# A local and pooled attention with a dense pair behind it: the new form from pair 8, with work moved between engines

## The chip, the cores and the metric

The kernel runs on one core of a Trainium2 chip. TensorE (PE in the profile; its weight loads are PEld) multiplies matrices, VectorE (DVE) and GpSimd (POOL) work elementwise, ScalarE (ACT) does copies and functions, and SyncE (SP) issues the DMAs. The metric is the time of one execution on the device in microseconds, as the median of three runs.

## The reference

There are 8 batches with 8 heads, 576 positions and head size 64. Two attentions are computed and added, and their sum, laid out as 4608 tokens of 512 features, goes through two matrix products with an elementwise function between them.

```python
q_d = q.reshape(B, H, Sd, factor, D).mean(axis=3)   # factor 4: 144 pooled positions; k_d, v_d alike
out_d = sm_attn(q_d, k_d, v_d)                      # softmax attention over the pooled positions
out_up = np.repeat(out_d, factor, axis=2)
mask = np.abs(pos[:, None] - pos[None, :]) < factor # a band of 7 positions
out_local = np.matmul(attn, v)                      # softmax of q k^T / 8 inside that band
x = (out_up + out_local) as [4608, 512]             # token by head and feature
h = x @ w_in;  g = h - np.tanh(h);  out = g @ w_out # 512 -> 2048 -> 512
```

## The kernel before

**Tiling.** Two heads of one batch make a pair; there are 32 pairs, four to a batch, and a batch is a block of 576 tokens. `attention(p)` handles a pair. The local attention works on five tiles of about 112 queries by 128 keys; the pooled attention on 5 groups of 32 pooled positions. For each pair, in order:

- loads of q, k and v (`load_qk`, `load_v`), two or four DMAs on SP, into four and five buffers;
- casts to bf16: `qr` (L443, one per head, on VectorE, ScalarE or GpSimd) and `vw` (L383);
- the transposition of q and k into `qk`, features on partitions. In the old form (`TIN` is 'pe') nine TensorE transposes (L466) into the score bank `ps_ts`, and two copies out of it (L474, ScalarE or VectorE). In the new form (`TIN` is 'dma') one DMA transpose (L448) from `qr` to `qT`, and two reorders of `qT` (L455, ScalarE);
- the pooled q and k: two additions, `half` (L486) and `qkd` (L495);
- the scores (L504) and pooled scores (L526), in two steps in the score bank, or where `MERGE` holds in one step over the score bank and the product bank `ps_ox`;
- exponents (L544, L555, L558) and, from pair 4, masks (L548 for 912 columns, L562 for 240);
- the products with V (L573) and pooled V (L579) into `ps_ox`, reciprocals and normalising (L588, L590) into `ln`;
- the way into `xT`, features on partitions again. In the old form (`XOUT` is 'pe') twelve TensorE products (L601, L604) and one copy (L632). In the new form one DMA transpose (L607) and a join of two additions (L619, L623).

`pool_v` pools V for two pairs: five products (L398, L400) and a copy (L405).

**The dense part.** `mm1` computes 128 of the 2048 inner features for 512 tokens (even blocks) or 320 (odd blocks): four products over the four head pairs (L662), tanh on ScalarE (L670) into `u`, and a subtraction on VectorE (L673) into `gT`. `mm2` multiplies `gT` with `w_out` (L690); a finished tile of 128 tokens is copied to `y` (L704) and stored (L707). `dense(kb)` interleaves `mm1` of block kb with `mm2` of block kb - 1; for kb 1 all of `mm2(0)` goes first. Block 0's attention runs by itself; from then on the attention of later pairs runs between the dense products.

**PSUM.** Eight banks: `ps_ts` (scores) and `ps_ox` (products), two banks each; in block 0 a second pair of the same, `ps_ts1` and `ps_ox1`, and after block 0 in their place four separate dense banks `ps_hy`.

**What sets the order.** Every step is recorded as an operation with an engine (or a choice of engines), a cost in ns, the keys that it reads and writes, and a priority. `Program.order` is a list planner: it starts on each engine the operation with the lowest priority number among those that are ready, and takes for a choice the engine that is free first. On SP at most eight DMAs are in flight. A result counts as ready for another engine after a latency (`LAT`: 230 ns from TensorE, 1800 ns from a DMA). Operations with priorities from `SPARE[0]` = 119 (pairs from 12, since the priority is ten times the pair) get a further margin: 600 ns ahead of TensorE, 1500 ns behind a DMA. TensorE's dense products have priority 5000 and fill what attention leaves free. The instructions are then issued on each engine in this order; what the planner took too short becomes a wait. Where the plan shows a longer idle time of TensorE in block 0, warm-up products (L824) on a zero tile are put in.

The constants that decide the forms stand at the end of the kernel:

```python
EARLY, BIASED = 12, 4
TIN = ['pe'] * EARLY + ['dma'] * (NPAIR - EARLY)
MERGE = [False] * EARLY + [True] * (NPAIR - EARLY)
XOUT = ['pe'] * EARLY + ['dma'] * (NPAIR - EARLY)
```

Of the kernel before, what the change touches and what calls it, by code (L numbers as in the profile page):

```python
# [8 lines left out]
FP32 = mybir.dt.float32  # L9
BF16 = mybir.dt.bfloat16  # L10
AF = mybir.ActivationFunctionType
ALU = mybir.AluOpType
PSUM = bass.MemoryType.PSUM


class Program:
# [8 lines left out]
    SPARE = 119, {"PE": 600, "ACT": 0, "DVE": 0, "DMA": 1500}  # L25
# [140 lines left out]
def kernel(  # L166
# [13 lines left out]
    NP = H // 2  # L180
    NPAIR = B * NP
# [54 lines left out]
    ps_hy = []  # L236


    early = ExitStack()
    psum_e = early.enter_context(tc.tile_pool(name="psum_e", bufs=1, space=PSUM))  # L240
    ps_ts1 = fixed("ps_ts1", [128, 2, 512], FP32, pool=psum_e)
    ps_ox1 = fixed("ps_ox1", [128, 2, 512], FP32, pool=psum_e)

    def dense_banks():
        early.close()
        pool = ctx.enter_context(tc.tile_pool(name="psum_d", bufs=1, space=PSUM))
        ps_hy.extend(fixed("ps_hy", [128, 512], FP32, 4, pool=pool))
# [141 lines left out]
    def pool_v(hb):  # L389

        w = hb % NVW
        pri = 20 * hb - 1
        bank, keys = (ps_ox, ["ox"]) if 2 * hb < NP else (ps_ts, [("ts", 0)])
        pv = bank[:, 0, :].rearrange("p (w c) -> p w c", w=2)

        def mm():
            for t in range(4):
                T.matmul(pv[32 * t:32 * t + 32, 0, :], pick[:, 0:32],  # L398
                         vw[w][:, :, t, 0:64], start=True, stop=True)
            T.matmul(pv[:, 1, :], pick[:, 32:160], vw[w][:, :, 4, 0:64],  # L400
                     start=True, stop=True)
        P.fresh.add(len(P.ops))
        op("PE", 350, mm, reads=[("vw", w, 0), ("vw", w, 1), "pick"],
           writes=keys, pri=pri)
        op("ACT", 470, lambda: A.copy(  # L405
            out=vd[w][:, :, :, 0:64],
            in_=pv.rearrange("p w (h d) -> p w h d", d=D)),
           reads=keys, writes=[("vd", w)], pri=pri)


    def attention(p):
# [27 lines left out]
        else:  # L439
            for hh in range(2):  # L440
                dst = qr[s][:, :, hh]
                srt = qkn[sn][:, hh].rearrange("p (a d) -> p a d", d=D)
                P.choice([(eng, ns, lambda dst=dst, srt=srt, fn=fn: fn(out=dst, in_=srt))  # L443
                          for eng, ns, fn in any3],
                         reads=[("qkn", sn, 0), ("qkn", sn, 1)],
                         writes=[("qr", s, hh)], pri=pri - 12)
        if TIN[p] == 'dma' and LOAD[p] == 'row':
# [6 lines left out]
            for i in range(2):  # L454
                op("ACT", 1080, lambda i=i: A.copy(  # L455
                    out=full[:, i].rearrange("p (g a) -> p g a", a=A9),
                    in_=qT[s][:, :, i::2].rearrange("p a g -> p g a")),
                   reads=[("qT", s)], writes=[("qk", s, i)], pri=pri)
# [88 lines left out]
        if not biased:  # L547
            op("DVE", 700, lambda: V.tensor_tensor(  # L548
            out=e1, in0=e1,
            in1=mask[:, 0:456].unsqueeze(1).to_broadcast([128, 2, 456]),  # L550
            op=ALU.mult), reads=["mask"], writes=[("E", s, 0)], pri=pri)
# [9 lines left out]
        if not biased:  # L561
            op("DVE", 300, lambda: V.tensor_tensor(  # L562
            out=e2v, in0=e2v,
            in1=mask[:, 456:576].unsqueeze(1).to_broadcast([128, 2, 120]),
            op=ALU.mult), reads=["mask"], writes=[("E", s, 1)], pri=pri)


# [38 lines left out]
        if XOUT[p] == 'dma':  # L606
# [21 lines left out]
            P.choice([("DVE", 800, lambda: join(V)), ("POOL", 1300, lambda: join(GP))],  # L628
# [8 lines left out]
    slots = [0, 1, 2, 3]  # L637
# [13 lines left out]
    def mm1(kb, i):  # L651
        t0, n, parts = span(kb)
        fc, g, c0 = i // parts, kb % 2, n * (i % parts)
        slot, us = take(), un[0] % 3
        un[0] += 1
        bs = sorted({(t0 + c0) // S, (t0 + c0 + n - 1) // S})

        def mm(part):
            if not ps_hy:
                dense_banks()  # L660
            for dc in range(2 * part, 2 * part + 2):
                T.matmul(ps_hy[slot][:, 0:n], w_in_sb[:, dc, fc * 128:(fc + 1) * 128],  # L662
                         xT[dc][:, t0 + c0:t0 + c0 + n],
                         start=(dc == 0), stop=(dc == N_DC - 1))
        for part in range(2):
            op("PE", 27 * n // 32, lambda part=part: mm(part),
               reads=[("w_in", fc // 4, c) for c in range(4)] +
               [("x", b, j) for b in bs for j in range(NP)],
               writes=[("hy", slot)], pri=5000)
        op("ACT", 90 + 76 * n // 100, lambda: A.activation(  # L670
            out=u[us][:, 0:n], in_=ps_hy[slot][:, 0:n], func=AF.Tanh),
           reads=[("hy", slot)], writes=[("u", us)], pri=-1)
# [3 lines left out]
           reads=[("hy", slot), ("u", us)], writes=[("gT", g, fc)], pri=-1)  # L676
# [4 lines left out]
    def mm2(kb, i):  # L681
# [16 lines left out]
        if part == 3:  # L698
# [5 lines left out]
            op("ACT", 480, lambda: A.copy(out=y[ys], in_=ps_hy[slot]),  # L704
               reads=[("hy", slot)], writes=[("y", ys)], pri=-1)
# [3 lines left out]
               reads=[("y", ys)], writes=[("yq", ys)], pri=-1)  # L709
# [15 lines left out]
    EARLY, BIASED = 12, 4  # L725
# [3 lines left out]
    XOUT = ['pe'] * EARLY + ['dma'] * (NPAIR - EARLY)  # L729
# [3 lines left out]
    LATE = 8  # L733
    T_QK, T_QKN, T_V, T_W, NEARLY = 840, 1350, 690, 2850, NP
# [121 lines left out]
```

## Time and profile before

| | |
|---|---|
| runs (us) | 338.45, 337.45, 338.14; median 338.14 |
| profiled execution (us) | 339.43, of which the span is 337.70 |
| granted TensorE clock | 1.00 |
| busy in the span (us) | TensorE 323.9, ScalarE 244.0, VectorE 213.4, GpSimd 130.8 |
| DMA | 58.15 MB, mean 172 GB/s |

The profile's page gives busy times, slices of the span, the chain of work that ended last, and groups of instructions with their idle time before them and what ended it. A row of a window shows the stretch, its length, and then per engine the busy time and the number of instructions (PE, PEld, DVE, ACT, POOL). A row of the chain is start, length, what ran. A row of the timeline is start, length, engine, line, operation, tiles, form, and in brackets the idle time before it with what ended it. A matmul's length includes its passage through the array; the distance between two starts is what it holds the engine.

### The profile page before, as it was taken

Reading aid. Unit: us, or ns where it says so; the run is one execution under the profiler, and the core shown is the slowest. Engines: PE = TensorE matmul, PEld = TensorE weight load, DVE = VectorE, ACT = ScalarE, POOL = GpSimd, SP = SyncE. Lnnn points to the kernel's source line nnn. Section 1 sums busy time; section 2 is a strip of 40 time slices with the busy share of each in tenths; the row PEclk is TensorE's granted clock in tenths of the full one; section 3 lists DMA queues with packets and bytes.
Section 4 is the critical chain, followed back from the end, with each engine's and each line's share of the span. In section 5 each row is a group of like instructions: output and inputs, shape, how many; then the busy total and the mean of one; then the engine's idle time right before and its main releaser. Section 6 shows DMA issues by size and latency. Waiting matters only on the chain.

```text
span 337.7 us, 7262 instructions
## 1 busy us (share of the span) xinstructions
PE 323.9 (96%) x2736; PEld 179.2 (53%) x2736; DVE 213.4 (63%) x401; ACT 244.0 (72%) x434; POOL 130.8 (39%) x176
## 2 busy tenths in 40 slices
PE   6898999989999999999799999999999999999995
PEld 2464455557664454566465445565664444665542
DVE  6577784558886788678578776786764333455200
ACT  3786896489998988998799999998654334554311
POOL 5644655574444464365375655645110000000000
PEclk9999999999999999999999999999999999999999
DMA  7999999866689999999999974453220100100021
GB/s 211 321 391 324 358 386 321 243 189 163 152 237 188 222 216 255 206 211 245 216 244 234 240 144 99 95 105 76 58 61 31 63 32 33 60 34 31 33 92 64
DMA packets 102979, 58.15 MB, mean 172 GB/s; under 512 B 86048, under 2 KB 86048, under 8 KB 102944
## 3 DMA queue, kind: packets, MB, share of 16 engines
q1 hardware_dynamic: 102944, 57.69, 65.0%
q8 instruction: 21, 0.34, 0.4%
q14 instruction: 14, 0.11, 0.1%
HBM read 37.75 MB, written 9.44 MB: 140 GB/s over the span
## 4 chain that ended last, share of the span: by engine, by line
PE 83%; ACT 5%; DVE 4%; DMA 4%; issue 1%; POOL 1%; SPq 0%; ACTq 0%; POOLq 0%
PE ps_hy L690 36%; PE ps_hy L662 33%; PE ps_ts L504 3%; PE ps_ox L573 3%; PE ps_ox L579 2%; ACT qk L474 2%; DVE qk L474 2%; PE ps_ts L466 2%; DMA lT<-ln 1%; DMA vst<-in_v_dram 1%; DMA qkn<-in_k_dram 1%; PE ps_ts L398 1%; PE ps_ts L400 1%; PE ps_ox L526 1%; PE ps_ox L604 1%
## 5 line engine op out<-in xcount | busy, mean ns | idle before, releaser
L662 PE MATMUL ps_hy<-xT,w_in_sb 128*128 128x320 bf16 (+1 forms) x768 | 147.0, 326 | 2.8 <-DVE gT L673 1.9
L690 PE MATMUL ps_hy<-w_out_sb,gT 128*128 128x512 bf16 x576 | 144.2, 379 | 0.0
L673 DVE TENSOR_TENSOR gT<-ps_hy,u 128x320 bf16<-128x320 f32 (+1 forms) x192 | 102.6, 552 | 59.2 <-ACT u L670 57.6
L670 ACT ACTIVATE u<-ps_hy 128x320 f32<-128x320 f32 (+1 forms) x192 | 92.3, 501 | 45.9 <-PE ps_hy L662 41.4
L662 PEld LDWEIGHTS <-w_in_sb 128*128 128x128 bf16 x768 | 72.3, 98 | 56.4 <-issue 3.1
L690 PEld LDWEIGHTS <-gT 128*128 128x128 bf16 x576 | 54.1, 98 | 53.9
L486 POOL TENSOR_TENSOR half<-qk 128x576 f32<-128x576 bf16 x31 | 36.1, 1166 | 40.5 <-ACT qk L455 25.3
L455 ACT COPY qk<-qT 128x576 bf16<-128x576 bf16 x40 | 48.1, 1219 | 0.0
L383 POOL CAST vw<-vst 128x640 bf16<-128x640 f32 x30 | 21.9, 734 | 40.4 <-PE ps_ox L573 40.1
L544 ACT ACTIVATE E<-ps_ts 128x912 bf16<-128x912 f32 x32 | 29.8, 932 | 9.1 <-PE ps_ts L504 7.5
L704 ACT COPY y<-ps_hy 128x512 f32<-128x512 f32 x36 | 21.3, 593 | 20.1 <-PE ps_hy L690 20.0
L590 DVE TENSOR_TENSOR ln<-ps_ox,r 128x896 bf16<-128x896 f32 x32 | 34.9, 1090 | 1.0
L443 POOL CAST qr<-qkn 128x576 bf16<-128x576 f32 x34 | 24.3, 727 | 20.8 <-PE ps_ts L466 16.8
L548 DVE TENSOR_TENSOR E<-E,mask 128x912 bf16<-128x912 bf16 x28 | 20.9, 748 | 10.4 <-ACT E L544 10.0
L495 POOL TENSOR_TENSOR qkd<-half 128x320 bf16<-128x320 f32 x28 | 21.7, 776 | 1.5
L573 PE MATMUL ps_ox<-vw,E 128*128 128x65 bf16 x320 | 19.3, 194 | 0.0
L573 PEld LDWEIGHTS <-E 128*128 128x128 bf16 x320 | 16.2, 98 | 5.6
L579 PE MATMUL ps_ox<-vd,E 128*128 128x65 bf16 x256 | 18.0, 193 | 0.1
L504 PEld LDWEIGHTS <-qk 64*128 64x128 bf16 x320 | 9.4, 95 | 15.8 <-issue 14.8
L588 DVE RECIPROCAL r<-ps_ox 128x14 f32<-128x14 f32 x32 | 7.7, 241 | 15.4 <-PE ps_ox L579 15.4
L504 PE MATMUL ps_ts<-qk 64*128 64x112 bf16 (+1 forms) x280 | 14.9, 216 | 1.0 <-DVE qk L474 1.0
L474 ACT COPY qk<-ps_ts 128x512 bf16<-128x512 bf16 (+1 forms) x14 | 10.2, 744 | 6.4 <-DVE qk L474 3.9
(75 smaller groups left out, 262.9 us busy)
## 6 DMA issues: line engine op xcount, KB each, us to landing
vst<-in_v_dram SPq DMA_DIRECT2D x64, 160.0 KB, 4.4
qkn<-in_q_dram SPq DMA_DIRECT2D x32, 288.0 KB, 4.1
qkn<-in_k_dram SPq DMA_DIRECT2D x32, 288.0 KB, 4.4
out_dram<-y SPq DMA_DIRECT2D x36, 256.0 KB, 2.3
gT<-in_moe_w_in_dram SPq DMA_DIRECT2D x4, 1024.0 KB, 10.0
xT<-in_moe_w_out_dram SPq DMA_DIRECT2D x8, 256.0 KB, 5.2
gT<-in_moe_w_out_dram SPq DMA_DIRECT2D x2, 1024.0 KB, 8.3
qT<-qr SPq DMA_TRANSPOSE x20, 3.5
```

The lines of the kernel that those rows point to most:

```text
L443: P.choice([(eng, ns, lambda dst=dst, srt=srt, fn=fn: fn(out=dst, in_=srt)) for eng, ns, fn in any3], reads=[("qkn", sn, 0), ("qkn", sn, 1 ...
L455: op("ACT", 1080, lambda i=i: A.copy(out=full[:, i].rearrange("p (g a) -> p g a", a=A9), in_=qT[s][:, :, i::2].rearrange("p a g -> p g a") ...
L486: eng.tensor_tensor(out=half, in0=four[:, :, :, 0:2], in1=four[:, :, :, 2:4], op=ALU.add)
L504: T.matmul(out, qk[s][rows, 1, KW * t:KW * t + 128], qk[s][rows, 0, Q0[t]:Q0[t] + NQ[t]], start=not biased, stop=not biased or t >= 3)
L544: op("ACT", 820, lambda: A.activation(out=e1, in_=ps[:, :, 0:456], func=AF.Exp, scale=SCALE), reads=ts, writes=[("E", s, 0)], pri=pri)
L573: T.matmul(po[:, hh, 65 * t:65 * t + 65], E[s][:, c:c + 128], vw[w][:, 2 * jj + hh, t, :], start=True, stop=True)
L579: T.matmul(po[:, hh, o:o + 65], E[s][:, c + GW * i:c + GW * i + 128], vd[w][:, i, 2 * jj + hh, :], start=(i == 0), stop=(i == 1))
L590: op("DVE", 1010, lambda: V.tensor_tensor(out=ln[s].rearrange("p n (h d) -> p h n d", d=D), in0=blocks[:, :, :, 0:64], in1=r[s].unsqueeze( ...
L662: T.matmul(ps_hy[slot][:, 0:n], w_in_sb[:, dc, fc * 128:(fc + 1) * 128], xT[dc][:, t0 + c0:t0 + c0 + n], start=(dc == 0), stop=(dc == N_DC ...
L670: op("ACT", 90 + 76 * n // 100, lambda: A.activation(out=u[us][:, 0:n], in_=ps_hy[slot][:, 0:n], func=AF.Tanh), reads=[("hy", slot)], writ ...
L673: op("DVE", 70 + 105 * n // 100, lambda: V.tensor_tensor(out=gT[g][:, fc, c0:c0 + n], in0=ps_hy[slot][:, 0:n], in1=u[us][:, 0:n], op=ALU.s ...
L690: T.matmul(ps_hy[slot], gT[g][:, fc, ts * 128:ts * 128 + 128], w_out_sb[:, fc, :], start=(fc == 0), stop=(fc == N_FF - 1))
```

## The change

The new form begins at pair 8 instead of 12; pairs 11 and 15, each the last of its block, keep or get the TensorE way into `xT`. Work is given to other engines by lists of alternatives: from pair 16 the joins and the casts of q and k stand on GpSimd alone; the reorders of pairs below 16 may go to VectorE; small masks from pair 4 may go to GpSimd; the y copies may go to VectorE. The y stores get a priority ahead of all other issues (-60 for -1). The planner's margin begins at priority 159 (pairs from 16). The V pooling of pairs 4 to 7 goes to the product bank. The dense banks are no longer tiles of their own: they are views of `ps_ts1`, `ps_ox1` and, for the first products only, `ps_ts`. The first four groups of block 0's `mm1` are cut into pieces of two, one and one products, and each product depends on the heads that it reads, no longer on all of them; the latter holds for all blocks.

```diff
-    SPARE = 119, {"PE": 600, "ACT": 0, "DVE": 0, "DMA": 1500}
+    SPARE = 159, {"PE": 600, "ACT": 0, "DVE": 0, "DMA": 1500}
...
+    ps_ts1 = fixed("ps_ts1", [128, 2, 512], FP32, pool=psum)
+    ps_ox1 = fixed("ps_ox1", [128, 2, 512], FP32, pool=psum)
+    ps_hy = [t[:, i] for t in (ps_ts1, ps_ox1, ps_ts) for i in range(2)]
+    shared = [("ts1", 0), ("ts1", 1), "ox1", "ox1", ("ts", 0), ("ts", 1)]
...
-        bank, keys = (ps_ox, ["ox"]) if 2 * hb < NP else (ps_ts, [("ts", 0)])
+        bank, keys = (ps_ox, ["ox"]) if not MERGE[2 * hb] else (ps_ts, [("ts", 0)])
...
-                          for eng, ns, fn in any3],
+                          for eng, ns, fn in any3[2 * (p >= CASTS):]],
...
+                P.choice([("ACT", 1080, lambda put=put: put(A.copy))] +
+                         [("DVE", 650, lambda put=put: put(V.tensor_copy))][:p < REORD],
+                         reads=[("qT", s)], writes=[("qk", s, i)], pri=pri)
...
-            P.choice([("DVE", 800, lambda: join(V)), ("POOL", 1300, lambda: join(GP))],
+            P.choice([("DVE", 800, lambda: join(V))][:p < JOIN] +
+                     [("POOL", 1300, lambda: join(GP))],
...
-    slots = [0, 1, 2, 3]
+    slots = [2, 3, 0, 1]
...
+        slot, us = (0, 1, 4, 5)[i] if (first := kb == 0 and i < 4) else take(), un[0] % 3
+        keys = [("hy", slot)] + [shared[slot]] * (kb == 0 and i < 6)
...
-        for part in range(2):
-            op("PE", 27 * n // 32, lambda part=part: mm(part),
+        for dcs in ((0, 1), (2,), (3,)) if first else ((0, 1), (2, 3)):
+            op("PE", 27 * n // 64 * len(dcs), lambda dcs=dcs: mm(dcs),
                reads=[("w_in", fc // 4, c) for c in range(4)] +
-               [("x", b, j) for b in bs for j in range(NP)],
-               writes=[("hy", slot)], pri=5000)
+               [("x", b, j) for b in bs for j in dcs],
+               writes=keys, pri=5000)
...
-            op("ACT", 480, lambda: A.copy(out=y[ys], in_=ps_hy[slot]),
-               reads=[("hy", slot)], writes=[("y", ys)], pri=-1)
+            P.choice([(eng, ns, lambda fn=fn: fn(out=y[ys], in_=ps_hy[slot]))
+                      for eng, ns, fn in YOUT],
+                     reads=[("hy", slot)], writes=[("y", ys)], pri=-1)
...
-               reads=[("y", ys)], writes=[("yq", ys)], pri=-1)
+               reads=[("y", ys)], writes=[("yq", ys)], pri=-60)
...
-    EARLY, BIASED = 12, 4
+    EARLY, BIASED = 8, 4
...
-    XOUT = ['pe'] * EARLY + ['dma'] * (NPAIR - EARLY)
+    XOUT = ['pe' if p < EARLY or p in (11, 15) else 'dma' for p in range(NPAIR)]
...
+    YOUT = [("ACT", 480, A.copy), ("DVE", 600, V.tensor_copy)]
+    JOIN, CASTS, REORD = 16, 16, 16
+    MASK1 = [[("DVE", 700, V.tensor_tensor)]] * 2
+    MASK2 = [[("DVE", 300, V.tensor_tensor)], [("DVE", 300, V.tensor_tensor), ("POOL", 600, GP.tensor_tensor)]]
```

The two masks are now choices too: `MASK1` names VectorE alone, as before, and `MASK2` adds GpSimd from pair 4.

More of the change, by code (lines that the diff above doesn't have):

```diff
@@ L454, in attention, with put @@
             for i in range(2):
[L455 to L458, printed above, removed]
+                def put(fn, i=i):
+                    fn(out=full[:, i].rearrange("p (g a) -> p g a", a=A9),
+                       in_=qT[s][:, :, i::2].rearrange("p a g -> p g a"))
+                P.choice([("ACT", 1080, lambda put=put: put(A.copy))] +
+                         [("DVE", 650, lambda put=put: put(V.tensor_copy))][:p < REORD],
+                         reads=[("qT", s)], writes=[("qk", s, i)], pri=pri)
         elif TIN[p] == 'pe':
@@ L547, in attention @@
         if not biased:
[L548 to L551, printed above, removed]
+            P.choice([(eng, ns, lambda fn=fn: fn(
+                out=e1, in0=e1, in1=mask[:, 0:456].unsqueeze(1).to_broadcast([128, 2, 456]),
+                op=ALU.mult)) for eng, ns, fn in MASK1[p >= NP]],
+                reads=["mask"], writes=[("E", s, 0)], pri=pri)
         yield
@@ L561, in attention @@
         if not biased:
[L562 to L565, printed above, removed]
+            P.choice([(eng, ns, lambda fn=fn: fn(
+                out=e2v, in0=e2v, in1=mask[:, 456:576].unsqueeze(1).to_broadcast([128, 2, 120]),
+                op=ALU.mult)) for eng, ns, fn in MASK2[p >= NP]],
+                reads=["mask"], writes=[("E", s, 1)], pri=pri)
         def outs():
@@ L653, in mm1, with mm @@
         fc, g, c0 = i // parts, kb % 2, n * (i % parts)
-        slot, us = take(), un[0] % 3
+        slot, us = (0, 1, 4, 5)[i] if (first := kb == 0 and i < 4) else take(), un[0] % 3
         un[0] += 1
+        keys = [("hy", slot)] + [shared[slot]] * (kb == 0 and i < 6)
         bs = sorted({(t0 + c0) // S, (t0 + c0 + n - 1) // S})
[L658 to L661, printed above, removed]
+        def mm(dcs):
+            for dc in dcs:
                 T.matmul(ps_hy[slot][:, 0:n], w_in_sb[:, dc, fc * 128:(fc + 1) * 128],
@@ L675, in mm1 @@
             op=ALU.subtract),
-           reads=[("hy", slot), ("u", us)], writes=[("gT", g, fc)], pri=-1)
+           reads=keys + [("u", us)], writes=[("gT", g, fc)], pri=-1)
     ycur = {}
```

11 lines of the change are left out of this document (1 added, 10 removed).

## The prediction

> **What bounds the kernel.** I read the page first, then the stages, the chain of waits, and single stretches of the timeline. From the page:
>
> ```profile
> span 337.7 us, 7262 instructions
> PE 323.9 (96%) x2736; PEld 179.2 (53%) x2736; DVE 213.4 (63%) x401; ACT 244.0 (72%) x434; POOL 130.8 (39%) x176
> PE 83%; ACT 5%; DVE 4%; DMA 4%; issue 1%; POOL 1%; SPq 0%; ACTq 0%; POOLq 0%
> ```
>
> TensorE is busy for 96% of the span, and 83% of the chain that ended last is its own work. By stages (after the engines: granted clock, DMA share, GB/s):
>
> ```profile
> 71.20:98.50 27.30, 26.43 (x316) 19.15 (x315) 22.89 (x49) 25.40 (x55) 12.38 (x16) 1.00 0.74 199
> 98.50:160.00 61.50, 61.50 (x548) 33.07 (x547) 47.95 (x85) 55.65 (x92) 32.99 (x39) 1.00 1.02 217
> 170.00:248.00 78.00, 78.00 (x719) 43.04 (x717) 57.50 (x102) 69.55 (x119) 40.95 (x49) 1.00 0.61 139
> 248.00:334.00 86.00, 85.94 (x457) 44.39 (x454) 32.12 (x59) 34.55 (x69) 0.00 (x0) 1.00 0.13 46
> ```
>
> From 98.5 us TensorE never rests, but for one hole at 162 us; work taken off it after that is time saved. From 71.2 to 98.5 us (the first product of block 1, beside pairs 8 to 11) ScalarE is busy 25.40 of 27.30 us too: there both must lose work. A merged pair costs TensorE little:
>
> ```profile
> 102.88 0.31 PE ps_ts L504 x8
> 103.19 0.05 PE ps_ox L504 x2
> 103.24 0.14 PE ps_ox L526 x4
> ...
> 242.93 0.31 PE ps_ts L504 x8
> ```
>
> These are the scores of pair 12 (0.50 us) and the first of pair 31: (242.93 - 102.88) / 19 = 7.37 us per pair.
>
> **The change, part by part.**
>
> (a) *New form for pairs 8 to 11.* They lose the nine transposes on TensorE (L466), and pairs 8, 9 and 10 the way back (L601, L604); pair 15 gets a way back. Prices, from the timeline of TensorE:
>
> ```profile
> 86.64 0.22 PE L601 MATMUL ps_ox<-ident,ln 120*128 120x120 bf16 x1
> ...
> 87.38 0.68 PE L466 MATMUL ps_ts<-ident,qr 128*128 128x128 bf16 x9
> 87.89 1.52 PE L662 MATMUL ps_hy<-xT,w_in_sb 128*128 128x320 bf16 x10
> ```
>
> A way back holds TensorE 87.38 - 86.64 = 0.74 us, the transposes 87.89 - 87.38 = 0.51. So 4 x 0.51 + (3 - 1) x 0.74 = 3.5 us. Most of it lies in the stage where ScalarE is as full, so its load there counts:
>
> ```profile
> L455 ACT COPY qk<-qT 128x576 bf16<-128x576 bf16 x40 | 48.1, 1219 | 0.0
> L443 ACT CAST qr<-qkn 128x576 bf16<-128x576 f32 x14 | 9.5, 681 | 2.8 <-DMA qkn<-in_k_dram 2.7
> L632 ACT CAST xT<-ps_ox 128x576 bf16<-128x576 f32 x5 | 3.3, 658 | 0.3 <-PE ps_ox L604 0.3
> L474 ACT COPY qk<-ps_ts 128x512 bf16<-128x512 bf16 (+1 forms) x14 | 10.2, 744 | 6.4 <-DVE qk L474 3.9
> ```
>
> In the order of the new kernel this stage has no L474 copy on ScalarE (four now), no L443 cast (two), one L632 for three, and four L455 reorders for two: -4 x 0.744 - 2 x 0.681 - 2 x 0.658 + 2 x 1.219 = -3.2 us. The cover shrinks with the work, so I take all of 3.5.
>
> VectorE gets one reorder of each of these pairs (9 of 48 by the order). No row shows that there: its plain cast of as many elements takes 0.745 us (row below), and with ScalarE's ratio of 1219 / 681 it would be 1.33. I take 0.8 as nearer to the row itself; 4 in the stage beside 22.89 busy of 27.30, less its L474 and L443, still fit.
>
> (b) *Waits that go with the old form* in pairs 8 to 11:
>
> ```profile
> 68.39 0.29 PE L398 MATMUL ps_ts<-vw,pick 128*32 128x256 bf16 x4 [0.65 <-ACT qk L474]
> 74.06 0.23 PE L504 MATMUL ps_ts<-qk 64*128 64x120 bf16 x2 [0.30 <-DVE qk L474]
> 80.25 0.38 PE L466 MATMUL ps_ts<-ident,qr 128*128 128x128 bf16 x4 [0.27 <-ACT qk L474]
> 89.70 0.23 PE L504 MATMUL ps_ts<-qk 64*128 64x120 bf16 x2 [0.29 <-DVE qk L474]
> ```
>
> Each waits for a copy out of the score bank that the new form does not make: 1.5 us. What is late next stands in (f).
>
> (c) *Joins on GpSimd from pair 16.* The hole at 162 us, by the chain and TensorE's timeline:
>
> ```profile
> 158.09 4.80 DMA lT<-ln
> ...
> 162.92 0.85 DVE xT L619
> ```
> ```profile
> 164.64 0.70 PE L662 MATMUL ps_hy<-xT,w_in_sb 128*128 128x320 bf16 x4 [1.92 <-DVE gT L673]
> ```
>
> VectorE stood behind a join that waited for a transposed tile; the subtractions behind it freed no bank, and TensorE lost 1.92 us. With that join on GpSimd the subtractions go on: -1.9, with 0 as the other end. GpSimd then waits instead; behind it stand the first sums and casts of later pairs.
>
> (d) *Block 0 head by head.*
>
> ```profile
> 27.31 0.23 PE L601 MATMUL ps_ox<-ident,ln 120*128 120x120 bf16 x1 [0.29 <-DVE ln L590]
> ...
> 28.97 2.75 PE L662 MATMUL ps_hy<-xT,w_in_sb 128*128 128x512 bf16 x12 [0.85 <-DVE xT L632]
> ...
> 36.64 0.29 PE L398 MATMUL ps_ts<-vw,pick 128*32 128x256 bf16 x4 [0.54 <-POOL vw L383]
> ```
>
> In the new order four products of heads 0 to 3 stand ahead of the last way back, where warm-up products and the 0.29 us wait stand now, and two more behind it, ahead of those that need the last head: 6 x 0.22 (2.75 / 12 = 0.23 a product, pipelined) = 1.3 us. The wait at 36.64 may take part of it back: it hangs on GpSimd's cast behind pair 4's sums, and these follow pair 4's transposes, which come earlier by less. I take 0.9, ends 0 and 1.3.
>
> (e) *The rest at nothing.* y copies: 18 of 36 go to VectorE; TensorE does not wait for one now. y stores ahead of other issues, and the planner's margin now from pair 16, only change the order; the V pooling of pairs 4 to 7 in the product bank costs what it costs in the score bank. SP gets four more L448 and two more L607 transposes, past loads that run up to four pairs ahead; the DMA share is 0.74 in the stage where most are added. Their landings now:
>
> ```profile
> DMA to landing us min/median/max: 3.2/3.5/5.6
> ```
>
> That row is of L448, issue to landing; by the planner's figures it counts on 1300 + 50 + 1300 + 1800 ns = 4.45 us, so most land in time.
>
> (f) *New waits.* Pairs 8 to 15 are planned without the 600 ns and 1500 ns that pairs from 12 have now, so products follow exponents closely, as in pairs 4 to 11. Four joins of pairs 10 to 14 stay on VectorE. Bounds: 0, or 0.65 us (the longest in (b)) for each of eight pairs and 1.92 for each of four joins, 12.9. I take 0.3, the usual row of (b), for the pairs and 0.5 for the joins together: +2.9.
>
> *Sum.* -3.5 - 1.5 - 1.9 - 0.9 + 2.9 = -4.9 us. The profiled execution took 339.43 us (span 337.70 and 1.73 around it), 1.29 over the median of the runs, 338.14. So 334.5 against the one and **333.2 us** against the other.
>
> **GpSimd's price.** Rows for what it gains and has:
>
> ```profile
> L486 POOL TENSOR_TENSOR half<-qk 128x576 f32<-128x576 bf16 x31 | 36.1, 1166 | 40.5 <-ACT qk L455 25.3 <-ACT qk L474 5.6 <-DVE qk L474 5.4
> L443 POOL CAST qr<-qkn 128x576 bf16<-128x576 f32 x34 | 24.3, 727 | 20.8 <-PE ps_ts L466 16.8 <-DMA qkn<-in_k_dram 3.4 <-DMA qT<-qr 0.6
> L383 POOL CAST vw<-vst 128x640 bf16<-128x640 f32 x30 | 21.9, 734 | 40.4 <-PE ps_ox L573 40.1 <-DMA vst<-in_v_dram 0.3
> L495 POOL TENSOR_TENSOR qkd<-half 128x320 bf16<-128x320 f32 x28 | 21.7, 776 | 1.5
> L623 POOL TENSOR_TENSOR xT<-lT 128x336 bf16<-128x336 bf16 x11 | 9.7, 881 | 0.0
> L619 POOL TENSOR_TENSOR xT<-lT 128x240 bf16<-128x240 bf16 x11 | 7.2, 652 | 8.1 <-DMA lT<-ln 8.1
> L443 DVE CAST qr<-qkn 128x576 bf16<-128x576 f32 x16 | 11.9, 745 | 0.3 <-DMA qkn<-in_k_dram 0.3
> L619 DVE TENSOR_TENSOR xT<-lT x9: 398/416/1207, 116.9 to 255.3; 128x240 bf16<-128x240 bf16 x9
> ```
>
> By the order it gains 20 casts, 22 small masks (taken as L619, the same size, 0.652) and 7 joins: 14.5 + 14.3 + 10.7 = 39.6 us on 130.8. Per pair from 16: 2 x 0.727 + 0.734 + 1.166 + 0.776 + 0.652 + 1.533 = 6.3 us of 7.37. It fits by 1.1 us.
>
> The same join on VectorE took 398 to 1207 ns (the last row, min/median/max), so something held it for up to 0.8 us. The Trainium skill, "SBUF — State Buffer", section "SBUF: two separate sides", says that VectorE and GpSimd share a port pair under an exclusive lock, and that the later one blocks for a whole instruction when VectorE reads two SBUF inputs. The trace agrees in size: the excess is about one GpSimd instruction. By that rule the masks left on VectorE and the GpSimd work would delay each other more often in the new kernel, which speaks for the second rival.
>
> **The rivals.**
> - *The stage at 71.2 keeps its length* (ScalarE and VectorE hand on too slowly, or the reorder costs 1.33). Then (a) and (b) save next to nothing there and (f) eats the hole: 338.14 - 0.9 = 337.2. For it: ScalarE's 25.40 of 27.30. Against: the 3.2 us that it loses.
> - *GpSimd becomes the bound* from pair 16. Its idle time ahead of L486 and L619 (25.3 us for ScalarE's reorder, 8.1 for landings, over 20 pairs: 1.7 per pair) harms nobody now. If that stays while its work is 6.3, a pair takes 8.0 us, 0.6 over 7.37; over 16 pairs 9.6 us: 333.2 + 9.6 = 342.8, slower. It decides from 0.3 us per pair (4.9 / 16). Against: waits shrink where an engine is late.
> - *Transposes collide with loads* (landings of 5.6 for 3.5 us where the share is 1.02): two or three holes of 1.9: 333.2 + 5.7 = 338.9.
> - *No new waits* in (f): 333.2 - 2.9 = 330.3.
>
> **How the numbers follow.** Forecast 0.58 (its own range 330.8 to 335.5), the stage 0.13, GpSimd 0.17, colliding transposes 0.05, no new waits 0.07. A time within 0.3% (1 us) cannot be told from no change. Faster: 0.58 + 0.07 + half of the stage's = 0.71; slower: 0.17 + most of the collisions = 0.21; within: 0.08. The range 329.8 to 340.0 reaches down to the best sum, (d) at 1.3 and (f) at 0 (338.14 - 8.2 = 329.9), and takes in the collisions and the mild part of GpSimd's case.
>
> **What would show it.** (a), (b): the first product of block 1 lasts 24 to 25 us, with no wait for a copy from ps_ts. (c): no VectorE join at 160 us and no hole over 1 us behind one. (d): products of block 0 before 27.3 us. (f): waits of 0.3 us ahead of L573 in pairs 8 to 15. GpSimd: about 170 us busy; if its idle time still ends on the reorders while TensorE waits for L504, the forecast is wrong.

## The result: 407 us for 338, and the profile after

The changed kernel takes 407.23 us in the median (407.16 to 407.31), the kernel before on the same chip 337.89 (337.45 to 338.45): a ratio of 1.205, 95% interval 1.203 to 1.207. Forecast were 333.2 us, in a range up to 340.0. The loss is 69 us, and no rival came near it.

The page after, the lines that answer to those shown of before:

```profile
span 405.6 us, 7126 instructions
PE 332.3 (82%) x2633; PEld 176.1 (43%) x2674; DVE 213.2 (53%) x381; ACT 227.5 (56%) x400; POOL 165.9 (41%) x232
PE 56%; DVE 18%; ACT 17%; issue 6%; DMA 2%; POOL 0%; SPq 0%; ACTq 0%; DVEq 0%; POOLq 0%
PE ps_ts L682 13%; PE ps_ts L654 12%; PE ps_ox L654 12%; PE ps_ox L682 11%; DVE gT L665 11%; ACT u L662 9%; DVE y L696 2%; ACT qk L448 2%; DVE ln L582 2%; ACT y L696 2%; PE ps_ts L498 1%; ACT qk L468 1%; DVE qk L468 1%; PE ps_ox L565 1%; PE ps_ts L460 1%
```

VectorE and ScalarE have no more work than before: 213.2 us (213.4) and 227.5 (244.0); GpSimd has 165.9 (130.8), as forecast ("about 170"). But TensorE, 96% busy before, stands at 82%, and its share of the chain fell from 83% to 56%. In its place came the subtraction (L665, 11%) and the tanh (L662, 9%) of the dense part, which were not in the list of lines of the chain before:

```profile
PE ps_hy L690 36%; PE ps_hy L662 33%; PE ps_ts L504 3%; PE ps_ox L573 3%; PE ps_ox L579 2%; ACT qk L474 2%; DVE qk L474 2%; PE ps_ts L466 2%; DMA lT<-ln 1%; DMA vst<-in_v_dram 1%; DMA qkn<-in_k_dram 1%; PE ps_ts L398 1%; PE ps_ts L400 1%; PE ps_ox L526 1%; PE ps_ox L604 1%
```

In the changed kernel the dense products are L654 and L682 (L662 and L690 before).

The stages (after the engines: granted clock, DMA share, GB/s):

```profile
78.13:114.61 36.48, 29.47 (x290) 18.15 (x291) 27.45 (x51) 25.60 (x54) 23.56 (x31) 1.00 0.91 216
114.61:180.00 65.39, 56.15 (x494) 29.83 (x501) 42.66 (x70) 46.18 (x77) 37.69 (x50) 1.00 0.88 208
190.00:279.00 89.00, 76.64 (x658) 40.76 (x669) 49.37 (x83) 63.36 (x105) 49.80 (x68) 1.00 0.50 112
295.72:401.82 106.10, 83.48 (x398) 39.29 (x405) 29.90 (x54) 28.01 (x56) 0.00 (x0) 1.00 0.09 33
```

and the last of them as it was before, for the same work (from the 145th tanh to the last copy into `y`):

```profile
256.16:334.02 77.86, 77.78 (x408) 39.72 (x406) 26.80 (x48) 30.95 (x61) 0.00 (x0) 1.00 0.12 45
```

The last two rows are the pure dense stage, with no attention, nothing on GpSimd and a DMA share of 0.09: 106.1 us for 77.9, and VectorE, ScalarE and TensorE have nearly the same instructions (48 tanh and 48 subtractions each, 405 weight loads for 406, 14 y copies for 13). So 28 us, four tenths of the loss, arise where none of the moved work runs but those copies. What is different there is only where the dense banks lie: views of the two-bank tiles `ps_ts1` and `ps_ox1` for four tiles of their own. Three microseconds of it in the timeline (start, length, engine, line, operation, tiles; in brackets the idle time before and what ended it):

```profile
340.77 0.38 PE L682 MATMUL ps_ts<-w_out_sb,gT 128*128 128x512 bf16 x1
341.24 0.44 ACT L662 ACTIVATE u<-ps_ts 128x320 f32<-128x320 f32 x1 [0.60 <-PE ps_ts L682]
341.73 0.59 PE L682 MATMUL ps_ts<-w_out_sb,gT 128*128 128x512 bf16 x2 [0.59 <-ACT u L662]
...
342.16 0.98 PE L654 MATMUL ps_ox<-xT,w_in_sb 128*128 128x320 bf16 x6
342.43 0.49 DVE L665 TENSOR_TENSOR gT<-ps_ts,u 128x320 bf16<-128x320 f32 x1 [1.26 <-PE ps_ts L682]
343.24 0.44 ACT L662 ACTIVATE u<-ps_ox 128x320 f32<-128x320 f32 x1 [1.55 <-PE ps_ox L654]
343.73 0.43 PE L654 MATMUL ps_ox<-xT,w_in_sb 128*128 128x320 bf16 x2 [0.59 <-ACT u L662]
```

A group of L682 products is in the middle of its sum in one bank of a tile. The tanh that reads the *other* bank of that tile waits for the product just issued; then the next product waits for that tanh, 0.59 us; then the subtraction waits for the next products, 1.26 us, though its tanh ended at 341.68. Engines that before worked side by side on two banks now take turns. Before, in the same stage, the tanh at 289.95 reads one bank while the products from 289.75 fill another, and nobody waits:

```profile
289.75 1.03 PE L690 MATMUL ps_hy<-w_out_sb,gT 128*128 128x512 bf16 x4
...
289.95 0.44 ACT L670 ACTIVATE u<-ps_hy 128x320 f32<-128x320 f32 x1
...
290.62 1.25 PE L662 MATMUL ps_hy<-xT,w_in_sb 128*128 128x320 bf16 x8
```

The Trainium skill, "PSUM — Partial Sum Buffer", section "PSUM bank collisions raise a hardware error", says that two engines on different banks run clean, and that semaphores should guard PSUM bank by bank. The rows of before agree: the chip does not ask for these waits. They must then come with the program, as semaphore waits put in tile by tile; the experiments test this.

### The profile page after: what moved, and what is told of

The parts are those of the page before. It is cut to its first block, busy times and chain, and to the rows that moved or that the text cites. A ratio compares the mean times of both kernels' runs of the same rounds, so it can differ in the third digit from the quotient of the medians.

```text
span 405.6 us, 7126 instructions
## 1 busy us (share of the span) xinstructions
PE 332.3 (82%) x2633; PEld 176.1 (43%) x2674; DVE 213.2 (53%) x381; ACT 227.5 (56%) x400; POOL 165.9 (41%) x232
## 4 chain that ended last, share of the span: by engine, by line
PE 56%; DVE 18%; ACT 17%; issue 6%; DMA 2%; POOL 0%; SPq 0%; ACTq 0%; DVEq 0%; POOLq 0%
PE ps_ts L682 13%; PE ps_ts L654 12%; PE ps_ox L654 12%; PE ps_ox L682 11%; DVE gT L665 11%; ACT u L662 9%; DVE y L696 2%; ACT qk L448 2%; DVE ln L582 2%; ACT y L696 2%; PE ps_ts L498 1%; ACT qk L468 1%; DVE qk L468 1%; PE ps_ox L565 1%; PE ps_ts L460 1%
## 5 line engine op out<-in xcount | busy, mean ns | idle before, releaser
L654 PEld LDWEIGHTS <-w_in_sb 128*128 128x128 bf16 x768 | 72.5, 97 | 97.2 <-issue 47.1
L654 PE MATMUL ps_ts<-xT,w_in_sb 128*128 128x320 bf16 (+1 forms) x387 | 80.2, 326 | 19.2 <-ACT u L662 7.8
L665 DVE TENSOR_TENSOR gT<-ps_ts,u 128x320 bf16<-128x320 f32 (+1 forms) x97 | 53.3, 557 | 75.2 <-ACT u L662 41.1
L682 PEld LDWEIGHTS <-gT 128*128 128x128 bf16 x576 | 54.7, 97 | 87.2 <-issue 37.2
L654 PE MATMUL ps_ox<-xT,w_in_sb 128*128 128x320 bf16 (+1 forms) x370 | 76.8, 323 | 16.3 <-DVE gT L665 6.3
L682 PE MATMUL ps_ox<-w_out_sb,gT 128*128 128x512 bf16 x277 | 73.5, 379 | 14.6 <-ACT u L662 8.5
L665 DVE TENSOR_TENSOR gT<-ps_ox,u 128x320 bf16<-128x320 f32 (+1 forms) x95 | 51.7, 554 | 62.6 <-ACT u L662 33.4
L662 ACT ACTIVATE u<-ps_ts 128x320 f32<-128x320 f32 (+1 forms) x97 | 47.4, 494 | 64.7 <-PE ps_ts L654 41.3
L682 PE MATMUL ps_ts<-w_out_sb,gT 128*128 128x512 bf16 x271 | 72.5, 379 | 12.6 <-ACT u L662 5.6
L662 ACT ACTIVATE u<-ps_ox 128x320 f32<-128x320 f32 (+1 forms) x95 | 45.6, 490 | 52.4 <-PE ps_ox L654 28.7
L448 ACT COPY qk<-qT 128x576 bf16<-128x576 bf16 x39 | 46.3, 1199 | 0.0
L435 POOL CAST qr<-qkn 128x576 bf16<-128x576 f32 x54 | 37.8, 712 | 4.9 <-DMA qkn<-in_k_dram 4.0
L556 POOL TENSOR_TENSOR E<-E,mask 128x240 bf16<-128x240 bf16 x22 | 15.8, 719 | 31.0 <-ACT E L549 29.5
```

Of the source, the lines that this page charges most:

```text
L448: fn(out=full[:, i].rearrange("p (g a) -> p g a", a=A9), in_=qT[s][:, :, i::2].rearrange("p a g -> p g a"))
L662: op("ACT", 90 + 76 * n // 100, lambda: A.activation(out=u[us][:, 0:n], in_=ps_hy[slot][:, 0:n], func=AF.Tanh), reads=keys, writes=[("u", ...
L665: op("DVE", 70 + 105 * n // 100, lambda: V.tensor_tensor(out=gT[g][:, fc, c0:c0 + n], in0=ps_hy[slot][:, 0:n], in1=u[us][:, 0:n], op=ALU.s ...
L682: T.matmul(ps_hy[slot], gT[g][:, fc, ts * 128:ts * 128 + 128], w_out_sb[:, fc, :], start=(fc == 0), stop=(fc == N_FF - 1))
```

## The experiments

Theory after the result: accesses to one PSUM tile are ordered with each other, whichever bank they touch, and the views made two dense banks share a tile. Rivals: the moved work (GpSimd, VectorE, SP); the view itself; the chip's own PSUM access.

### Own banks again, and the views alone

`own_banks` is the changed kernel with four one-bank tiles for the dense part as before (and so without the head by head start, which needs the views). `views_only` is the kernel before with nothing but the views:

```diff
-        ps_hy.extend(fixed("ps_hy", [128, 512], FP32, 4, pool=pool))
...
+    ps_ts1 = fixed("ps_ts1", [128, 2, 512], FP32, pool=psum)
+    ps_ox1 = fixed("ps_ox1", [128, 2, 512], FP32, pool=psum)
+    ps_hy = [t[:, i] for t in (ps_ts1, ps_ox1, ps_ts) for i in range(2)]
```

> The changed kernel, but the four dense banks are tiles of their own again (made when block 0's banks are given back), and with that block 0's first products start after the last head again. All other parts of the change stay. Theory T (the added time is waits between the two banks of one tile): the time falls to 331 to 337 us, GpSimd still about 165 us busy. Rival G (GpSimd's longer work bounds the pairs from 16) or rival M (the planner's missing margin for pairs 8 to 15): it stays above 380 us, since the casts, joins, masks and margins are the same.

> The kernel before, with one edit: the four dense banks are views of the two two-bank tiles of block 0. Theory T: it loses what the changed kernel loses or more, 390 to 425 us, with waits of TensorE on tanh and subtraction of the neighbour bank in the stage after 250 us, where no attention runs. Rivals G and M: 338 us, since neither GpSimd's work nor a margin is changed.

Measured: own_banks 339.10 us (335.91 to 341.72, and 338.5 without the highest of its ten runs; ratio 1.0025, 0.9992 to 1.0058); views_only 419.35 us (ratio 1.241, 1.239 to 1.244). The one edit makes a loss of 81 us by itself, and without it the changed kernel cannot be told from the kernel before, though it stays above the 331 to 337 us that I expected. The moved work is out as the main cause. The list of TensorE's waits in views_only (total us, times, longest; buffer numbers left out) is headed by the two shared tiles, where before all products of this line (L662) waited 2.8 us in total:

```profile
PE ps_ts L651 <- DVE gT L662: 9.3, 16, 0.9
PE ps_ox L651 <- DVE gT L662: 9.0, 16, 1.3
```

Differences from own_banks below are taken from 339.10 us; from 338.5 each is 0.6 us more where the other kernel is slower, and 0.6 less where it is faster.

### Other order of the slots

`alternate` takes the dense slots in the order 2, 0, 3, 1 for 2, 3, 0, 1, so that successive groups lie in different tiles (and keeps the first eight groups on the keys of the tiles).

```diff
-    slots = [2, 3, 0, 1]
+    slots = [2, 0, 3, 1]
```

> The changed kernel with another rotation of its four dense banks: 2, 0, 3, 1 in place of 2, 3, 0, 1, so that neighbours in time lie in different tiles. Theory T: the number of waits stays, but each is for work that lies one group further back, so the loss shrinks to between a third and two thirds: 360 to 385 us. Rivals G and M: 407 us, unchanged.

Measured: 411.19 us. My expectation was wrong: the order of the slots does not help. Whatever the order, each of the four banks shares its tile with another that is in use. That reading is argued from the timeline above, not shown by a run.

### One-bank views, and one shared pair

Two doses of the kernel before that leave the order of all engines as it is. In `one_bank_views` the dense banks are views too, but of four tiles of one bank each; in `one_pair_shared` two banks are own tiles and two are views of one tile `ps_hz`.

```diff
-        ps_hy.extend(fixed("ps_hy", [128, 512], FP32, 4, pool=pool))
+        ps_hy.extend(t[:, 0] for t in fixed("ps_hy", [128, 1, 512], FP32, 4, pool=pool))   # one_bank_views
...
+        ps_hy.extend(fixed("ps_hy", [128, 512], FP32, 2, pool=pool))                       # one_pair_shared
+        two = fixed("ps_hz", [128, 2, 512], FP32, pool=pool)
+        ps_hy.extend(two[:, i] for i in range(2))
```

> The kernel before, its four dense banks taken as views of four tiles of one bank each. Nothing else changes, the order of every engine least of all. Theory (accesses to one tile are ordered with each other, whatever bank they lie in): with one bank to a tile there is no neighbour to wait for, so 338 us. Rival (a view in itself is dear, by its access pattern or its tracking): the 81 us of the run with views alone come again, about 419 us, or at least a good part of them.

> The kernel before with two of its four dense banks as own tiles and the other two as views of one tile of two banks. Theory (waits between neighbours in a tile): half the groups have a neighbour, the other half have none and cover a part of what the first lose, so the loss is between a quarter and a half of the 81 us: 358 to 378 us. Rival (it needs all banks coupled, a chain through both tiles): under 350 us. Rival (any shared tile couples all of TensorE's order): over 400 us.

Measured: one_bank_views 337.85 us (ratio 0.9997, 0.9987 to 1.0008); one_pair_shared 381.85 us (ratio 1.130). A view costs nothing; two banks in one tile cost 44 us, four in two tiles 81. The 381.85 lies 4 us above my range. Both kernels give the engines the same order as before, so what was moved elsewhere is out for good. They also use the same four banks, the only ones left beside `ps_ts` and `ps_ox`, so the chip's own access to these is out too. That it is the framework that keeps the order by tile is inferred from this. TensorE's waits in one_pair_shared, from the same list, name the shared tile and leave the two own ones alone:

```profile
PE ps_hz L664 <- DVE gT L675: 10.3, 20, 1.5
PE ps_hz L692 <- ACT u L672: 6.4, 13, 0.7
PE ps_hz L664 <- ACT u L672: 6.3, 13, 0.7
PE ps_hz L692 <- DVE gT L675: 5.3, 10, 0.9
...
PE ps_hy L664 <- DVE xT L634: 0.8, 1, 0.8
```

The largest wait on `ps_hy` is one of 0.8 us, for an attention result. The cause of the 69 us is settled, but for the head by head start, which needs the views and was not tried without them; it acts before the 17th tanh, where the changed kernel is 3.7 us behind own_banks (78.13 us for 74.43, in the table below). What follows asks why the rest of the change did not give the 333 us that I forecast.

### The new form from pair 12 or 8, alone and with the y stores

`own_banks_early12` is own_banks with `EARLY` at 12 for 8. `pair8_alone` is the kernel before with the new form from pair 8 and nothing else (`EARLY` 8, `XOUT` as changed); `pair8_y_first` adds the y stores' priority. `own_banks_y_behind` is own_banks with that priority undone.

```diff
-               reads=[("y", ys)], writes=[("yq", ys)], pri=-1)     # before, pair8_alone, own_banks_y_behind
+               reads=[("y", ys)], writes=[("yq", ys)], pri=-60)    # after, own_banks, pair8_y_first
```

> As own_banks, but the new form starts at pair 12 again, with the way back on TensorE for pairs 0 to 11 and 15. It takes away the part that was priced at -3.5 - 1.5 us of TensorE work and waits, and adds one way back (0.74 us). If those terms were right, it is 4 to 6 us slower than own_banks; if the stage from 71 us keeps its length whatever the form, the two are within 1 us.

> The kernel before with the new form from pair 8 (pairs 11 and 15 keep or get the TensorE way back) and nothing else: planner margin, engines and tiles as before. Predicted terms (a) -3.5 and (b) -1.5 give 333 us. If the stage of the first product of block 1 keeps its length because ScalarE alone makes all reorders here (two more of 1.22 us for each of four pairs than the change leaves it in part to VectorE), 337 to 339 us.

> The new form from pair 8 alone (355.5 us) with the y stores first added, nothing else. The run without it loses some 24 us between 72 and 105 us, by waits for late transposes ahead of joins on VectorE and by one wait of TensorE for the copy into y behind a late store. If the late stores on SP are what starts it, 340 to 346 us. If the joins on VectorE and a clock of 0.50 behind the first holes are the larger part, 350 us or more.

> The changed kernel with own dense banks and the y stores at the priority they had before (-1 for -60), so behind loads and transposes that are ready. I priced the move of the stores at nothing: 338 to 340 us. If stores behind loads keep y buffers and with them dense banks (in the run of the new form alone, a y store landed 4 us late and TensorE waited 2.7 us for the copy into y), 342 us or more.

Measured: own_banks_early12 342.85 us, pair8_alone 355.52, pair8_y_first 338.11 (335.53 to 339.72), own_banks_y_behind 394.53. So the new form from pair 8 is worth 3.8 us where the other parts stand (342.85 - 339.10, just under the 4 to 6 that I expected; own_banks_early12 also has the V pooling of pairs 8 to 11 in the product bank) and costs 17.6 us alone, where I had expected 333 or 337 to 339 us. One priority takes all of that back, more than the 340 to 346 us that I expected, but gains nothing on the kernel before (ratio 0.9992, 0.9964 to 1.0019). Where it is missing, the changed kernel with own banks loses 55 us. I had priced that priority at nothing. SP's queue in own_banks_y_behind (L448, L607 transposes; L321, L351 loads; L710 y stores):

```profile
74.79 1.42 SPq L607 DMA_TRANSPOSE lT<-ln  x1
76.38 2.81 SPq L448 DMA_TRANSPOSE qT<-qr  x1
79.24 0.58 SPq L351 DMA_DIRECT2D vst<-in_v_dram  x1
...
145.77 1.18 SPq L351 DMA_DIRECT2D vst<-in_v_dram  x2
146.99 1.47 SPq L710 DMA_DIRECT2D out_dram<-y  x3
```

The first copy into `y` starts at 70.4 us, and SP issues no store until 146.99: loads have priority -30, transposes -50, stores -1, and with the transposes from pair 8 on (1.4 and 2.8 us in these rows) SP's queue is never empty. There are three y buffers; the fourth copy into `y` starts at 151.59 us, behind the stores, for 77.42 in own_banks. So no dense bank comes free, and attention runs by itself. In own_banks the same stores go out between the loads:

```profile
72.92 0.61 SPq L351 DMA_DIRECT2D vst<-in_v_dram  x1
73.64 0.92 SPq L710 DMA_DIRECT2D out_dram<-y  x2
74.61 0.50 SPq L351 DMA_DIRECT2D vst<-in_v_dram  x1
75.20 0.83 SPq L710 DMA_DIRECT2D out_dram<-y  x1
```

### GpSimd's part

`own_banks_old_engines` gives joins, casts and small masks back to the engines they had before. `margin_masks_vector`, run later, takes only the small masks back from GpSimd (in the kernel with the margin, below).

```diff
-    JOIN, CASTS, REORD = 16, 16, 16
+    JOIN, CASTS, REORD = 32, 32, 16      # own_banks_old_engines only
...
-    MASK2 = [[("DVE", 300, V.tensor_tensor)], [("DVE", 300, V.tensor_tensor), ("POOL", 600, GP.tensor_tensor)]]
+    MASK2 = [[("DVE", 300, V.tensor_tensor)], [("DVE", 300, V.tensor_tensor)]]
```

> The changed kernel with own dense banks, and joins, casts and small masks with the engines that they had before (from pair 16 no longer GpSimd alone, no small mask on GpSimd). If GpSimd costs the changed kernel what it gains elsewhere (second rival: the product of a pair waits 2.5 us for a small mask on GpSimd at 131 us), 334 to 337 us against 339.1. If the joins on GpSimd are worth the 1.9 us of term (c) and the rest is harmless, 340 to 342 us.

> Own banks, margin from pair 12, and the small masks on VectorE alone as before (GpSimd keeps joins and casts from pair 16). If small masks in GpSimd's queue hold products (waits of 0.4 to 2.5 us in the runs with own banks), 334.5 to 336 us against 336.9. If VectorE then stands in the way of the subtractions, 338 to 341 us; no difference within 1 us if the order alone decides.

Measured: own_banks_old_engines 342.12 us against 339.10; margin_masks_vector 340.66 against 336.90. The work on GpSimd is worth 3.0 us, the small masks alone 3.8 in the kernel with the margin; so no gain is left that the joins and casts can be shown to make. It does have the price I feared in (c): a join on GpSimd that waits holds what is queued behind it. In own_banks, on GpSimd and TensorE:

```profile
129.01 0.60 POOL L619 TENSOR_TENSOR xT<-lT 128x240 bf16<-128x240 bf16 x1 [3.41 <-DMA lT<-ln]
...
133.19 0.64 POOL L564 TENSOR_TENSOR E<-E,mask 128x240 bf16<-128x240 bf16 x1
```
```profile
133.89 0.23 PE L573 MATMUL ps_ox<-vw,E 128*128 128x65 bf16 x1 [2.38 <-POOL E L564]
```

The late tile stops GpSimd for 3.41 us, four operations stand between it and the mask, and the product with V waits 2.38 us for the mask. In that hole TensorE's granted clock falls to half and stays there for 3.4 us (third figure from the end):

```profile
133.62:137.04 3.42, 2.94 (x19) 1.66 (x21) 1.94 (x3) 0.46 (x1) 3.09 (x5) 0.50 1.36 193
```

### The margin, and the V pooling

`own_banks_margin` gives pairs 12 to 15 the planner's margin again; `margin_from_pair8` gives it to pairs 8 to 11 too; `margin_pool_back` is own_banks_margin with the V pooling of pairs 4 to 7 back in the score bank.

```diff
-    SPARE = 159, {"PE": 600, "ACT": 0, "DVE": 0, "DMA": 1500}
+    SPARE = 119, {"PE": 600, "ACT": 0, "DVE": 0, "DMA": 1500}    # own_banks_margin; 79: margin_from_pair8
...
-        bank, keys = (ps_ox, ["ox"]) if not MERGE[2 * hb] else (ps_ts, [("ts", 0)])
+        bank, keys = (ps_ox, ["ox"]) if 2 * hb < NP else (ps_ts, [("ts", 0)])    # margin_pool_back
```

> The changed kernel with own dense banks and the planner's margin from pair 12 again, as before (in the changed kernel from pair 16). Own banks gain 6.8 us on the kernel before between the first product of block 1 and the next stage and lose 6.8 us again between 101 and 162 us, where pairs 12 to 15 run. If that loss is term (f), new waits because those pairs are planned without margin, most of it goes: 333 to 335.5 us against 339.1. If it comes from GpSimd (a small mask held a product for 2.5 us) or from chance in the order, 338 to 341 us.

> Own banks, and the planner's margin from pair 8 (336.9 us with the margin from pair 12). Term (f) said 2.9 us for pairs 8 to 15 without margin; the margin on pairs 12 to 15 gave 2.2 us in the medians. If the margin is worth as much for pairs 8 to 11, 334 to 335.5 us. If the first product of block 1, which already gains, is bound by the work of its engines and not by waits, 336 to 338 us.

> As the run with own banks and the margin from pair 12 (336.9 us), with the V pooling of pairs 4 to 7 in the score bank again. That run is 3.0 us behind the kernel before at the seventeenth tanh (74.9 us), all of it from 29 to 37 us, where TensorE waits for casts and copies of pair 4 (0.9, 1.0 and 0.7 us) between groups of four dense products; with the pooling in the score bank twelve dense products stand between the same steps. If the moved pooling makes that loss, 334 to 335 us. If it comes from elsewhere (small masks and casts on GpSimd in these pairs), 336 to 338 us.

Measured: own_banks_margin 336.90 us (335.74 to 338.15; ratio 0.9969, 0.9951 to 0.9988), margin_from_pair8 337.40 (ratio 0.9989, 0.9978 to 0.9999), margin_pool_back 338.28 (ratio 1.0006, 0.9976 to 1.0036). The margin on pairs 12 to 15 is worth 2.2 us (I had expected a time of 333 to 335.5), on pairs 8 to 11 nothing. The pooling makes no loss: with it back, the 17th tanh starts at 74.41 us for 74.91. own_banks_margin has the lowest median here, 0.3% under the kernel before and 70 us under the changed one.

Where the time goes, by the start of the n-th of 192 tanh in the profiled executions (the 17th opens block 1's first product, the 49th block 2's); one_bank_views stands for the order of before, since its executed time is the usual one:

| tanh | one_bank_views | own_banks | own_banks_margin | after |
|---|---|---|---|---|
| 17th | 71.68 | 74.43 | 74.91 | 78.13 |
| 49th | 103.81 | 101.30 | 101.05 | 114.61 |
| 81st | 158.03 | 162.34 | 156.42 | 179.91 |
| 192nd | 314.99 | 317.54 | 312.85 | 381.61 |

```profile
74.43:101.30 26.87, 25.21 (x252) 16.45 (x252) 25.13 (x50) 20.41 (x46) 20.63 (x27) 1.00 1.08 253
101.30:162.34 61.04, 57.55 (x512) 31.00 (x520) 37.41 (x63) 47.77 (x81) 43.40 (x58) 0.97 1.12 241
```
```profile
74.91:101.05 26.14, 24.71 (x252) 16.39 (x251) 23.75 (x49) 23.59 (x52) 21.44 (x28) 1.00 1.08 246
101.05:156.42 55.37, 55.37 (x490) 29.62 (x488) 36.53 (x62) 42.96 (x74) 35.54 (x49) 1.00 1.07 244
```

The first fence is own_banks, the second own_banks_margin. The first product of block 1 falls from 32.13 us (103.81 - 71.68) to 26.87 and 26.14, but begins some 3 us later. From there to the 81st tanh own_banks loses 6.8 us (61.04 for 54.22), with the hole of 2.38 us and the half clock behind it (the mean of 0.97 in its row); own_banks_margin loses 1.2, with TensorE busy all of 55.37. Both lose about 3 us ahead of the 17th tanh.

## Why the prediction was wrong

**The step that failed is (e), "the rest at nothing".** It lists y copies, y stores, the planner's margin and the V pooling, and has no price for the edit that decided: the dense banks as views. The section on the change describes it in one sentence, and the prediction says nothing of it, as if it were a renaming: the same banks are used in the same number. What it changes is which accesses share a tile, and so which waits are put in: 81 us alone, 69 with the rest of the change.

A row for it stood in the prediction. In (b) the four transposes at 80.25 us wait 0.27 us for a ScalarE copy out of `ps_ts`. I read it as "a copy out of the score bank". On ScalarE that copy is

```profile
79.43 0.77 ACT L474 COPY qk<-ps_ts 128x640 bf16<-128x640 bf16 x1
```

640 columns are the first five planes, which lie in bank 0; the four transposes go into bank 1 (`ps[:, i]` with `i` 1). They share only the tile with it. Waits of that kind, 0.59 and 1.26 us in the timeline above, are what the dense part is full of now.

**Also in (e), and wrong: the y stores "only change the order".** I had named the queue (SP) and its cover, loads that run ahead, but not who stands behind whom: SP's spare time is what lets stores of the lowest rank out at all, and the transposes of pairs 8 to 11 use it up. The priority is worth 17 us beside pair8_alone and 55 in own_banks.

**(a) and (b), -5.0 us: the work fell as priced, the time did not fall with it.** The first product of block 1, in one_bank_views, pair8_y_first and own_banks_early12:

```profile
71.68:103.81 32.13, 31.24 (x359) 21.61 (x357) 25.49 (x53) 29.77 (x60) 16.31 (x21) 1.00 0.74 195
72.66:105.21 32.55, 28.10 (x284) 17.83 (x284) 24.99 (x52) 27.90 (x55) 17.52 (x23) 0.99 1.08 240
82.65:110.43 27.78, 25.73 (x292) 17.70 (x291) 25.67 (x51) 22.21 (x50) 21.52 (x27) 1.00 1.08 234
```

In pair8_y_first, with the new form and the stores' priority alone, TensorE's busy time falls by 3.1 us and the stage takes as long as before: TensorE now waits 1.9 us for a join on GpSimd, 1.1 for the normalising on VectorE and 1.4 for dense banks. In own_banks the stage is 5.3 us shorter, but that does not measure the form: in own_banks_early12, in the old form, it is 27.78 us too, with fewer of TensorE's products in it (292 for 359) and a later start. What the form is worth among the other parts is the 3.8 us of the medians; by the prices of (a) and (b) it would be 5.8 there (4 x 0.51 + 3 x 0.74 + 1.5, as own_banks_early12 has three ways back more). The reorder on VectorE, taken at 0.8 us, took this in own_banks:

```profile
L456 DVE COPY qk<-qT 128x576 bf16<-128x576 bf16 x11 | 8.6, 798 | 1.4 <-PE ps_ox L506 1.1 <-POOL vw L383 0.3
```

**(c), -1.9 us: not borne out.** The hole of 1.92 us at 162 us was that of one execution. With the same order, in one_bank_views, it is 0.44:

```profile
162.91 0.70 PE L662 MATMUL ps_hy<-xT,w_in_sb 128*128 128x320 bf16 x4 [0.44 <-DVE gT L673]
```

The profiled execution stood 1.29 us over the median, as the prediction says; this place, 1.48 us longer, accounts for it, and I counted it as a gain all the same. GpSimd's work did gain, 3.0 us together, but through the small masks, which I took for a cost; the joins were not tried by themselves. And the wait moved, as the row of 2.38 us above shows.

**(d), -0.9 us: open.** In the changed kernel the first three of these products start at 26.63 us, ahead of the last way back, and the first tanh at 29.59 us for 30.08 (29.83 in one_bank_views): a gain of 0.2 to 0.5 at that point. But a wait for a subtraction that the kernel before does not have there takes back more:

```profile
32.10 0.59 PE L654 MATMUL ps_ts<-xT,w_in_sb 128*128 128x512 bf16 x2 [1.69 <-DVE gT L665]
```

With own banks it was not tried. Nor is it settled why the kernels with own banks lose 3 us before the 17th tanh; the place of the V pooling is not the reason.

**(f), +2.9 us: near in size, other in shape.** Pairs 8 to 11 lost nothing without margin, pairs 12 to 15 6.8 us in one execution, 2.2 in the medians. But I had summed many short waits of 0.3 us behind exponents. Between the 49th and the 81st tanh of own_banks TensorE waits 2.7 us in two waits, both for a small mask on GpSimd, and the larger is the hole of 2.38.

**The rivals.** The stage at 71 us keeps its length where the form and the stores' priority stand alone, as the first rival has it (32.55 us for 32.13). GpSimd is not the bound: busy as forecast, and taking work from it makes the kernel slower. By the rule of the Trainium skill, "SBUF — State Buffer", section "SBUF: two separate sides", that VectorE and GpSimd share a port pair under an exclusive lock, more GpSimd work should have spoken for this rival; the runs show a net gain of 3.0 us, so whatever the two cost each other is less than what the move frees. Late transposes do cost something: the hole of 2.38 us in own_banks hangs on one. The times of own_banks spread over 4.6 us even without the highest, those of own_banks_early12 and of the kernel before beside them over 0.6 and 1.1; that the transposes make this spread was not tried. Without the views, and so without (d), the sum would have been 334.1 us (338.14 - 3.5 - 1.5 - 1.9 + 2.9); 336.9 to 339.1 is what the rest of the change gives.

## What to carry to other kernels

When an edit changes what shares a tile, price it as new waits: list for each tile which engine writes one part while another reads the other part, and look in the trace for a wait between two such parts; waits of 0.6 to 1.3 us at the hand-overs of the bounding engine made a quarter of this kernel's time (81 of 338 us). Before calling a priority free, ask what lets the lowest rank of that queue out today, and whether the change takes that gap away. And a hole that is in the profiled execution but not in the median is no gain to be had.

## What the runs showed of the hardware

When attention ran by itself in own_banks_y_behind, TensorE's granted clock fell to half and stayed there until the work was dense again (windows; the third figure from the end is the clock):

```profile
83.92:87.34 3.42, 1.16 (x21) 0.59 (x19) 1.80 (x3) 2.15 (x5) 2.92 (x4) 1.00 1.20 78
87.34:159.02 71.68, 32.79 (x382) 22.05 (x383) 38.72 (x53) 39.41 (x56) 55.16 (x70) 0.50 1.05 243
155.60:159.02 3.42, 3.42 (x24) 1.86 (x19) 1.87 (x4) 2.60 (x6) 0.00 (x0) 0.50 1.08 250
159.02:170.00 10.98, 10.02 (x112) 6.95 (x111) 8.59 (x20) 10.38 (x23) 8.33 (x12) 1.00 1.01 231
```

TensorE was busy for 34% of the 3.42 us before the fall (1.16 of 3.42), for 46% of the 71.68 us at 0.50, and for all of the 3.42 us before the rise. A single hole does the same in small: in own_banks, before the 3.42 us at 0.50 shown above, TensorE was busy for 38% (1.31 of 3.42):

```profile
130.20:133.62 3.42, 1.31 (x10) 0.59 (x8) 0.00 (x0) 2.81 (x4) 3.34 (x5) 1.00 0.99 299
```

The Trainium skill, "TensorE: Matmul & The Clock Gate", section "Part 1: The HAM clock gate", says that the clock is passed at half rate after an idle window and in full after a busy one; the trace agrees in both levels, though here TensorE was not idle before a fall but about a third busy. In the changed kernel, by contrast, TensorE was busy for 79% of the last stage (83.48 of 106.10), and the clock stayed at 1.00: that loss is waits, not a slower clock.
